# A fused attention and phase-mixer kernel: the first batch's exponentials transposed by TensorE instead of by DMA, and a new instruction order

## The chip, the cores and the metric

One core of a Trainium2 chip runs the whole program. The metric is the device time of one execution in microseconds (us). The engines are TensorE (PE in the rows, with its weight loads as PEld), VectorE (DVE), ScalarE (ACT), GpSimd (POOL) and SyncE (SP), whose queue here only issues DMAs.

## The reference

```python
# q, k, v: 8 batches x 8 heads x 576 x 64;  w_theta, w_ch: 512 x 512;  w_tok_r, w_tok_i: 576 x 576
scores = q @ k^T / sqrt(64)                      # row block i sees column blocks j <= i, blocks of 64
attn   = exp(scores - max) / (sum + 1e-9)
x      = attn @ v                                # per batch 576 x 512 after joining the heads
theta  = x @ w_theta
y      = w_tok_r @ (x * cos(theta)) + w_tok_i @ (x * sin(theta))
u      = x + y
out    = u + relu(u @ w_ch)
```

## The kernel before

The work is cut into some 3,400 parts: functions with the parts that they need, the PSUM banks that they take and the banks that they leave. `emit` calls them by a long list of numbers, `ORDER`; `BANKS` names a bank for each label that a part takes, and `PLACES` an engine (A, D or P for ACT, DVE, POOL) for each part that may run on several. Each engine works through its own instructions in this order, so a wait holds up all that stands behind it on that engine.

A batch has eight heads in four pairs; pair p holds heads 2p and 2p+1. A head's 576 query rows are five tiles: piece A is tiles 3, 2 and 4, piece B tiles 1 and 0, and for the first 16 heads the two pieces go separately, later as one. For the first three batches the scores are products of f32 operands (L589, `scores_wide` into two banks for each head, `scores_narrow` into one, and `scores_first`, L617, for tile 4), for the others three f16 products each.

A head then passes through: row maxima on DVE (L633); the bias `m` (L641, POOL or DVE); exponentials on ACT (L646) out of PSUM into an f32 tile `t` in SBUF, after which the score banks are free; `high`, a cast to f16 `p` (L431 on ACT, L433 on DVE or POOL); `low`, the rest t - p in f16 (L436, DVE or POOL); `turn`, a DMA transpose of both (L665, `pt<-p`, in SP's queue); the products with v (L680, PE); normalising on DVE (L692, L694, L698). `t` may be written again by the next pair when `low` has read it. DMAs (L686) join the halves of x; x is split (`xp`), transposed by DMA (L806) and multiplied with w_theta (L816, L819). The angles are reduced on ACT (L828) and DVE (L834, L440/L442), and one part, `sines`, turns a batch's angles into cosines and sines with six ACT instructions (L849, L851) between two ACT_TABLE_LOADs. Products with x (`z`, L860), their split into `zh` and `zl`, the token mix (L884), u (L893, L900), the channel mix (L907), relu (L913, L915), the sum (L923) and the store follow. All eight batches run interleaved: while one is mixed, the attention of the next is done.

The weights are loaded, scaled and split into high and low f16 parts during the first batch (lines L462 to L518). Loads of q, k and v (L772) stand in SP's queue among the transposes.

Of the kernel before, what the change touches and what calls it, by code (L numbers as in the profile page):

```python
# [12 lines left out]
F32 = mybir.dt.float32  # L13
# [20 lines left out]
HALVED = 8  # L34
WHOLE = 3

ORDER = [
# [191 lines left out]
    "DAAADAPPAPPPAPDPAPPDAPPPPPPDPPPPAPPPPPPDPPDDAPDADAPDDADDAAAADAAPPDAPPDDDDADPDAPDPADDDAPDPPDDPADPPDDDDAPDPPPPPDPP"  # L229
    "PADDADDPDPPDDADAAAA"  # L230
)

Part = namedtuple("Part", "f needs takes leaves on")


# [19 lines left out]
def attention_phase_mixer(  # L255
# [10 lines left out]
    nc = tc.nc  # L266
# [751 lines left out]
    def keys(name, n):  # L1018
        return [(name, n, x) for x in pieces(n)]
# [157 lines left out]
```

## Time and profile before

| | |
|---|---|
| time, median of 3 runs (lowest, highest) | 665.99 us (665.96, 668.66) |
| profiled execution: span | 668.2 us |
| busy PE | 615.9 us (92%) |
| busy DVE | 570.6 us (85%) |
| busy ACT | 508.4 us (76%) |
| busy POOL | 393.8 us (59%) |
| mean granted TensorE clock | 0.959 |

The page gives no separate own time for the profiled execution; its span of 668.2 us is 0.3% above the median of the runs, and only the run of 668.66 us could hold it. Sums below are made against the span. Busy shares are means over the whole execution; the stages, of which the first 124 us are very unlike the rest, are told apart in the rows below. In rows of a timeline the columns are start, duration, engine, line, operation, out<-in, shapes, count, and in brackets the idle time before it with what ended it.

### The profile page before, as it was taken

The page shows a single profiled execution, that of the slowest core. Times are in us where ns is not written, and L with a number is a line of the kernel's source. Part 1 is how long each engine was busy: PE and PEld are TensorE (multiplying, and loading weights), DVE is VectorE, ACT ScalarE, POOL GpSimd, SP SyncE. Part 2 cuts the span into 40 slices and gives each one's busy share as a digit, 9 for nine tenths or more (in the row PEclk, how much of TensorE's full clock was granted, in tenths as well). Part 3 has the DMA queues.
Part 4 walks back from the last instruction along what each step waited for, and adds up shares of the span by engine and source line. Part 5 has one row for each costly group of instructions (what it writes and reads, how often), then busy time and mean ns, then how long its engine had stood idle before and what let it go on. Part 6 is the DMA issues. An engine that isn't in the chain of part 4 may idle for free. (4 is left out here: it accounts for less than half of the span.)

```text
span 668.2 us, 18051 instructions
## 1 busy us (share of the span) xinstructions
PE 615.9 (92%) x7372; PEld 459.6 (69%) x7374; DVE 570.6 (85%) x1136; ACT 508.4 (76%) x776; POOL 393.8 (59%) x411
## 2 busy tenths in 40 slices
PE   5477796999999999999999998999999998999997
PEld 3155554876788578776778766875786586857775
DVE  4987897998998998989989889999998998846474
ACT  5997878776997998978998899889997986325111
POOL 4355564876575446564675748664777476673340
PEclk9578896999999999999999999999999998999999
DMA  8999999998989596989869897889797655840002
GB/s 347 381 235 231 207 165 196 248 197 147 233 197 214 126 242 122 194 170 183 220 169 169 164 222 164 192 169 202 186 207 156 120 89 117 172 82 1 19 36 88
DMA packets 268514, 116.57 MB, mean 174 GB/s; under 512 B 256016, under 2 KB 256016, under 8 KB 268432
## 3 DMA queue, kind: packets, MB, share of 16 engines
q1 hardware_dynamic: 268432, 115.43, 78.5%
q8 instruction: 57, 0.93, 0.6%
q14 instruction: 25, 0.20, 0.1%
HBM read 42.01 MB, written 9.44 MB: 77 GB/s over the span
## 5 line engine op out<-in xcount | busy, mean ns | idle before, releaser
L884 PEld LDWEIGHTS <-zh 128*128 128x128 f16 x1152 | 112.7, 98 | 30.4 <-issue 1.6
L884 PE MATMUL g<-wT_h,zh 128*128 128x288 f16 x405 | 115.9, 286 | 0.3 <-DVE xT L923 0.3
L884 PE MATMUL g<-wT_l,zh 128*128 128x288 f16 x405 | 115.8, 286 | 0.0
L884 PE MATMUL g<-wT_h,zl 128*128 128x288 f16 x405 | 115.8, 286 | 0.0
L680 PE MATMUL g<-v,pt 128*128 128x65 f16 x2880 | 104.8, 197 | 10.5 <-DVE xn L698 4.4
L680 PEld LDWEIGHTS <-pt 128*128 128x128 f16 x2880 | 101.0, 100 | 17.7 <-issue 9.6
L633 DVE TENSOR_REDUCE m<-s 128x1 f32<-128x576 f32 (+3 forms) x134 | 86.4, 668 | 12.0 <-PE s L596 11.8
L436 POOL TENSOR_TENSOR p<-t,p 128x512 f16<-128x512 f32 (+4 forms) x31 | 69.8, 2254 | 43.7 <-ACT p L431 26.5
L431 ACT CAST p<-t 128x1600 f16<-128x1600 f32 (+4 forms) x62 | 79.7, 1289 | 7.8 <-DMA pt<-p 6.8
L436 DVE TENSOR_TENSOR p<-t,p 128x1600 f16<-128x1600 f32 (+4 forms) x49 | 80.4, 1643 | 4.3 <-ACT p L431 3.8
L860 POOL TENSOR_TENSOR aa<-aa,xn 128x256 f32<-128x256 f32 (+1 forms) x63 | 51.5, 829 | 28.1 <-ACT aa L849 25.5
L816 PEld LDWEIGHTS <-xT 128*128 128x128 f16 x384 | 36.6, 98 | 43.8 <-DMA xT<-xp 2.4
L884 PEld LDWEIGHTS <-zl 128*128 128x128 f16 x576 | 56.4, 98 | 14.4 <-POOL m L641 0.4
L646 ACT ACTIVATE t<-s,m,size 128x576 f32<-128x576 f32 (+1 forms) x80 | 59.2, 777 | 8.1 <-POOL m L641 6.0
L907 PEld LDWEIGHTS <-wch_h 128*128 128x128 f16 x512 | 48.1, 98 | 14.7 <-issue 2.9
L633 DVE TENSOR_REDUCE m<-g 128x1 f32<-128x320 f32 (+2 forms) x154 | 53.5, 369 | 2.3 <-PE g L596 0.7
L646 ACT ACTIVATE t<-g,m,size 128x192 f32<-128x192 f32 (+2 forms) x100 | 49.2, 533 | 5.4 <-POOL m L641 3.5
L436 POOL TENSOR_TENSOR zl<-aa,zh 128x512 f16<-128x512 f32 (+1 forms) x38 | 44.7, 1181 | 12.9 <-PE g L617 6.9
L907 PE MATMUL g<-ul,wch_h 128*128 128x288 f16 x164 | 46.9, 286 | 2.8 <-DVE ul L900 2.8
L884 PE MATMUL s<-wT_l,zh 128*128 128x288 f16 x171 | 48.9, 286 | 0.0
L884 PE MATMUL s<-wT_h,zl 128*128 128x288 f16 x171 | 48.9, 286 | 0.0
L884 PE MATMUL s<-wT_h,zh 128*128 128x288 f16 x171 | 48.9, 286 | 0.0
(187 smaller groups left out, 1632.8 us busy)
## 6 DMA issues: line engine op xcount, KB each, us to landing
rv<-in_v SPq DMA_DIRECT2D x16, 768.0 KB, 5.3
rq<-in_q SPq DMA_DIRECT2D x16, 640.0 KB, 5.3
rk<-in_k SPq DMA_DIRECT2D x16, 576.0 KB, 5.5
out<-xT SPq DMA_DIRECT2D x32, 288.0 KB, 2.5
w_raw<-in_w_tok SPq DMA_DIRECT2D x5, 576.0 KB, 5.4
pt<-in_w_tok SPq DMA_DIRECT2D x4, 576.0 KB, 7.4
w_raw<-in_w_theta SPq DMA_DIRECT2D x4, 512.0 KB, 7.0
w_raw<-in_w_ch SPq DMA_DIRECT2D x4, 512.0 KB, 5.6
```

The lines of the kernel that those rows point to most:

```text
L431: nc.scalar.copy(out=out, in_=x)
L436: engine_of(on).tensor_tensor(out=out, in0=x, in1=y, op=ALU.subtract)
L633: nc.vector.tensor_reduce(out=self.m[:, i:i + 1], in_=self.scores_of(i), axis=AX.X, op=ALU.max)
L646: nc.scalar.activation(out=t_parts[self.hh][:, to:to + n], in_=self.scores_of(i), func=AF.Exp, scale=self.scales()[0], bias=self.m[:, NI + ...
L680: nc.tensor.matmul(o[:, i, :], lhsT=source[:, block, :], rhs=vv[:, slot, hh, :], start=first, stop=last)
L816: nc.tensor.matmul(g, lhsT=xT[:, xx + i, :], rhs=ww[:, dt, :], start=first, stop=last)
L860: engine_of(on).tensor_tensor(out=cd, in0=cd, in1=self.xns[dt][:, i0:i0 + ni, :], op=ALU.mult)
L884: nc.tensor.matmul(g, lhsT=zz[:, kk, cols], rhs=ww[:, kk, ts], start=(n == 0 and kk == k0 and nn == 0), stop=n == 4 and kk == k0 + ni - 1 ...
L907: nc.tensor.matmul(g[:, 0:HS], lhsT=ww[:, dt, e * P:(e + 1) * P], rhs=uu[:, dt, th * HS:(th + 1) * HS], start=dt == 0 and n == 0, stop=dt ...
```

## The change

For the eight heads of the first batch (`PE_TURNED = 8`) the casts, subtractions and DMA transposes of `high`, `low` and `turn` go (16, 16 and 16 of them). In their place stand `turn_up` (L670 after the change), which transposes the f32 exponentials in blocks of 128 x 128 on TensorE back into the head's own score banks, 8 blocks for piece A, 4 for B, and one more for tile 4 into a bank of its own (100 blocks in all); `turned_high` (20 casts from PSUM to the f16 `pt`, 19 on ACT, 1 on DVE) and `turned_low` (20 subtractions that read PSUM, all on DVE). The score banks of these heads are left by `turned_low`, not by the exponentials; `t` may be written again after the transposes. `sines` becomes six parts, and each part of `z` needs only the one or two whose result it reads. `ORDER`, `BANKS` and `PLACES` are new throughout.

```diff
+PE_TURNED = 8
...
 ORDER = [
-    8, 9, 158, 160, 335, 10, 11, 0, 1, 16, 17, 2, 56, 340, 364, 363, 372, 373, 374, 336, 339, 57, 40, 3, 350, 58,
...
-    t_parts = [const.tile([P, USED[hh]], F32, name=f"t{hh}") for hh in range(2)]
+    t_parts = [const.tile([P, NS[hh]], F32, name=f"t{hh}") for hh in range(2)]
+    nc.gpsimd.memset(t_parts[0][:, USED[0]:NS[0]], 0.0)
...
+        def turned_in(self, piece):
+            if piece == "4":
+                return bank_of["t4", self.n]
+            return self.pair.wide(self.hh) if piece == "A" else self.pair.narrow(self.hh)
+
+        def turn_up(self, piece):
+            x, to = t_parts[self.hh], self.turned_in(piece)
+            for j, c in enumerate({"A": range(CUT, CUT + 1024, P), "B": range(0, CUT, P), "4": [CUT + 1024]}[piece]):
+                nc.tensor.transpose(to[:, j * P:(j + 1) * P], x[:, c:c + P], ident)
...
+        def turned_high(self, piece, on):
+            x, hi, _ = self.turned_parts(piece)
+            copied(on, hi, x)
+
+        def turned_low(self, piece):
+            x, hi, lo = self.turned_parts(piece)
+            less("D", lo, x, hi)
...
-        def sines(self):
+        def sines(self, n):
...
-            for c, x, rows in ((a[:, 0:4, :], a[:, 0:4, :], slice(0, P)), (a[top, 4, left], a[top, 4, left], top),
+            if n in (0, 1):
+                steps = [(a[:, 2 * n:2 * n + 2, :], a[:, 2 * n:2 * n + 2, :], slice(0, P))]
...
-                    add(("e", n, i), step_of(h.exponentials, i), needs, leaves=leaves)
...
+                    add(("e", n, i), step_of(h.exponentials, i), needs, leaves=leaves if n >= PE_TURNED else ())
+                if n < PE_TURNED:
+                    for x in [piece] + ["4"] * (piece == "A" and hh == 0):
+                        done = [("e", n, i) for i in {"A": (3, 2), "B": (1, 0), "4": (4,)}[x]]
+                        add(("tp", n, x), step_of(h.turn_up, x), done, takes=[("t4", n)] if x == "4" else ())
+                        add(("th", n, x), step_of(h.turned_high, x), [("tp", n, x)] + w_free, on="AD")
+                        add(("tl", n, x), step_of(h.turned_low, x), [("th", n, x)],
+                            leaves={"A": [("s1", p, hh, k) for k in range(2)], "B": [("s2", p, hh)], "4": [("t4", n)]}[x])
...
-                    part("z", (hf, n, half), m.times_x, [("sines", b)], on="PD")
+                    part("z", (hf, n, half), m.times_x, [("sines", b, x) for x in ((0,), (3,), (1,), (4,), (2, 5))[n]], on="PD")
```

Before the first token mix, DVE's order also loses nine biases and eleven small operations on weights, sizes, v and x to other engines, and gains five products `z`.

On PE at the start of the program, between the first pair's scores and the second pair's, the order before goes from the first wide scores (in s0 and s1) through the mask straight to the second wide scores in the same banks:

```order
L596 MATMUL s0_109<-ones_119,mask_q_70 128x2x64
L596 MATMUL s1_110<-ones_119,mask_q_70 128x2x64
L589 MATMUL s0_109<-rk_154,rq_152 128x512
L589 MATMUL s1_110<-rk_154,rq_152 128x512
```

At the same place the order now has (t0 and t1 are the exponentials of the pair's two heads, g4 to g7 single banks):

```order
L595 MATMUL s1_111<-ones_120,mask_q_70 128x2x64
...
L670 MATMUL g4_112<-ident_r_79,t1_98 128x128 x4
L616 MATMUL g7_115<-rk_151,rq_153 128x64 x2
L670 MATMUL g6_114<-ident_r_79,t0_97 128x128 x4
...
L670 MATMUL s1_111<-ident_r_79,t1_98 128x128 x8
L670 MATMUL s0_110<-ident_r_79,t0_97 128x128 x8
L670 MATMUL g6_114<-ident_r_79,t0_97 128x128
L588 MATMUL s0_110<-rk_151,rq_153 128x512
L588 MATMUL s1_111<-rk_151,rq_153 128x512
```

The second pair's wide scores now stand behind 25 transposes and, through the banks, behind the casts and subtractions that read them.

In SP's queue, the program's first DMAs and the loads of q and k for the second half of the second batch stood so before (the numbers tell buffers apart; pt is what a DMA transpose of p writes):

```order
L462 DMA w_raw_128<-in_w_theta 128x1024
L772 DMA rq_152<-in_q 128x1280
L772 DMA rk_154<-in_k 128x1152
...
L806 DMA_TRANSPOSE xT_1124<-xp_1071 128x10x128
L665 DMA_TRANSPOSE pt10_105<-p1_100 128x16x128
L665 DMA_TRANSPOSE pt10_105<-p1_100 128x8x128
L772 DMA rq_1201<-in_q 128x1280
L772 DMA rk_1219<-in_k 128x1152
```

and stand so now, with nothing ahead of the first two and, between the start and the loads of rq_736 and rk_783, no transpose of any kind:

```order
L796 DMA rk_151<-in_k 128x1152
L796 DMA rq_153<-in_q 128x1280
L461 DMA w_raw_129<-in_w_theta 128x1024
...
L796 DMA rq_736<-in_q 128x1280
L710 DMA xn_709<-xn_709 64x64
L796 DMA rk_783<-in_k 128x1152
L710 DMA xn_709<-xn_709 64x64
L796 DMA rv_843<-in_v 128x1536
L830 DMA_TRANSPOSE xT_847<-xp_692 128x10x128
```

Both loads have moved from behind the transposes of the second batch's first pair to ahead of the first transpose of x.

On ACT the first batch's sines stood in one piece between two table loads:

```order
L849 ACT_TABLE_LOAD
L849 ACTIVATE aa<-aa,half_pi 128x2048
L849 ACTIVATE aa<-aa,half_pi 64x256 x2
L851 ACTIVATE rr<-rr 128x2048
L851 ACTIVATE aa<-rr 64x256 x2
L646 ACT_TABLE_LOAD
```

and now they stand between the same two loads in pieces, with two of the reductions (L439) among them:

```order
L881 ACT_TABLE_LOAD
L881 ACTIVATE rr<-rr 128x1024
L439 ACTIVATE aa<-rr 128x256
L439 ACTIVATE aa<-rr 128x512
L883 ACTIVATE aa<-aa,half_pi 128x1024
L881 ACTIVATE rr<-rr 128x1024
L883 ACTIVATE aa<-aa,half_pi 64x256 x2
L883 ACTIVATE aa<-aa,half_pi 128x1024
L881 ACTIVATE aa<-rr 64x256 x2
L645 ACT_TABLE_LOAD
```

A product `z` can follow each piece instead of the last one.

## Rows read from the trace of the kernel before

**Rows 1.** Stage, length, busy PE, PEld, DVE, ACT, POOL (instructions), clock, DMA share, GB/s.

```profile
0.00:40.00 40.00, 21.12 (x98) 13.09 (x101) 28.42 (x60) 29.95 (x52) 18.00 (x43) 0.75 0.95 338
40.00:80.00 40.00, 30.05 (x416) 23.22 (x413) 32.89 (x79) 32.82 (x58) 23.30 (x26) 0.83 1.18 235
80.00:124.00 44.00, 36.43 (x400) 25.02 (x401) 39.24 (x80) 34.75 (x56) 23.96 (x27) 0.81 0.90 190
124.00:300.00 176.00, 175.36 (x2218) 133.40 (x2217) 161.59 (x332) 148.75 (x225) 111.00 (x115) 1.00 0.91 187
300.00:420.00 120.00, 116.11 (x1538) 85.90 (x1537) 110.59 (x216) 107.78 (x160) 77.22 (x73) 1.00 0.83 185
420.00:560.00 140.00, 132.88 (x1725) 98.48 (x1724) 131.00 (x252) 119.92 (x176) 90.80 (x84) 0.99 0.78 157
```

**Rows 2.** PE's timeline up to the first token mix (L884).

```profile
7.61 0.87 PE L589 MATMUL g<-rk,rq 64*128 64x320 f32 x1 [7.61 <-DMA rk<-in_k]
...
23.76 4.11 PE L589 MATMUL s<-rk,rq 64*128 64x512 f32 x16 [7.17 <-ACT t L646]
...
106.59 4.11 PE L589 MATMUL s<-rk,rq 64*128 64x512 f32 x16 [3.43 <-DMA rk<-in_k]
...
118.89 2.17 PE L589 MATMUL s<-rk,rq 64*128 64x512 f32 x16
...
122.43 1.55 PE L680 MATMUL g<-v,pt 128*128 128x65 f16 x45
123.81 0.29 PE L884 MATMUL g<-wT_h,zh 128*128 128x288 f16 x1
```

**Rows 3.** SP's queue: starts, time taken to issue, and count.

```profile
0.74 0.40 SPq L462 DMA_DIRECT2D w_raw<-in_w_theta  x1
...
1.67 0.42 SPq L772 DMA_DIRECT2D rk<-in_k  x1
...
94.25 4.34 SPq L665 DMA_TRANSPOSE pt<-p  x2
99.28 0.42 SPq L772 DMA_DIRECT2D rk<-in_k  x1
```

**Rows 4.** Two other stretches, same columns as rows 1.

```profile
9.90:113.00 103.10, 74.50 (x757) 50.66 (x758) 88.30 (x192) 87.41 (x146) 55.11 (x57) 0.78 1.05 249
123.80:198.10 74.30, 73.88 (x909) 56.02 (x906) 68.80 (x142) 59.51 (x94) 52.25 (x54) 1.00 0.98 194
```

**Rows 5.** DVE's timeline, the last that the first token mix needs.

```profile
110.85 1.16 DVE L633 TENSOR_REDUCE m<-s 128x1 f32<-128x448 f32 x2 [3.57 <-PE s L596]
111.92 0.68 DVE L436 TENSOR_TENSOR p<-t,p 128x512 f16<-128x512 f32 x1
112.52 0.48 DVE L698 TENSOR_TENSOR xn<-g,r 128x320 f32<-128x320 f32 x1
```

**Rows 6.** Groups of DVE by shape, 0 to 124 us: busy time, mean ns.

```profile
L436 DVE TENSOR_TENSOR p<-t,p 128x1024 f16<-128x1024 f32 x4 | 5.0, 1249 | 0.1
L433 DVE CAST p<-t 128x1024 f16<-128x1024 f32 x2 | 1.4, 690 | 0.8 <-DMA pt<-p 0.8
L834 DVE SCALAR_TENSOR_TENSOR rr<-s,size,aa 128x512 f32<-128x512 f32 x1 | 0.7, 737 | 0.0
L641 DVE TENSOR_SCALAR m<-m 128x3 f32<-128x3 f32 x5 | 1.6, 326 | 0.1
L860 DVE TENSOR_TENSOR rr<-rr,xn 128x256 f32<-128x256 f32 x3 | 1.5, 505 | 0.0
```

**Rows 7.** ACT's timeline, first and last of the first batch's sines.

```profile
105.02 2.92 ACT L849 ACTIVATE aa<-aa,half_pi 128x2048 f32<-128x2048 f32 x3
...
109.89 0.85 ACT L851 ACTIVATE aa<-rr 64x256 f32<-64x256 f32 x2
```

**Rows 8.** PE's waits from 124 to 560 us: total, times, longest.

```profile
PE g L907 <- DVE ul L900: 2.8, 2, 2.6
PE s L907 <- ACT t L646: 2.5, 2, 1.9
```

More of the change, by code (lines that the diff above doesn't have):

```diff
@@ L34 @@
 HALVED = 8
+PE_TURNED = 8
 WHOLE = 3
 ORDER = [
[176 rows of a table removed]
[174 rows of a table added]
 ]
 BANKS = (
-    "4556164551001236001234501234601235601235401231001236501236401235401234601235601235601235601234501235401235401235"
-    "4012346012354012346012346012345012354012356012356012346012356012365012346012364012365012365246551650445606454041"
-    "6540151630666461566050425316646355451406665420444500465601466501605440544155446405425450164156455646416040451634"
-    "52245163452601620132435450513216524"
+    "6036634613301236460123451012346501235400123650123100123640123640123540123460123560123560123560123450123540123540"
+    "1235401234601235401234601234601234501235401235601235601234601235601236501234601236401236501236524650165044562445"
+    "1366654015041066656146605041531566625545056616403655450046560146652046315014405544561042543015410645564641503045"
+    "126452542562535304460316014405260435142"
@@ L220 @@
 )
 PLACES = (
-    "DAAPDAPAAADAAAAAAPDAPDAAPAAAAAPAAPAAPAAPAADAAPADAAAAPDPPPPDDDDAPPDAPPAPDDDDAPPDADPPPDAPPPPADADPAPPAPPPPAPADPPDDP"
-    "DDPPPDAPPAPPADPPDDPADPAPPADPAPADADPADDADPAPAPADDADPPAPPPDPPADPADAPADPADAADPADDAPAAPPADPAPAAADADPADPPADADPADAPADA"
-    "PPADAAADDDPAPAAADADDAPPPPPADDADAAPPAPDADAAPDPDPADAAPDADPPDAPAPADPADAAPDADPAPAAAPADPPDAAPPADPAPAAAPADPADAAAPADPDP"
-    "AAPPDDPAPAAPPAPPAPPPPPADDADPDAPADAPADDAAPPPDDDAPPPAPDPADPPAPPDAPPPAPDDAPPDAPPPPPPADPPDDPAADADAADADADAPPDAADADPPP"
-    "PDDPPPDPPPPAPPDAPDPADPPPPPPADPPADPPAPDADAPAPDAADAADDAAPAPAPDDDAAAAPDPPDPAPDDDPPDAPDPPDPPAPDPAPDPAPDDADPDPPPAPPDP"
@@ L227 @@
-    "PDAAADDDAAAPPPPPDDAAAADPDADPDAPPPPPDDPPPDPPPDAPPPAPDPAPPPAPDPPPPAPAPADADAAADDADAPAPAPPPDAAADDPAPPPPDPPAPPPAPPPAD"
-    "PPAPPDAPDPAPDDADPDPPPAPAPADADDDADADDAPADPPAPAADADPDPPPPPPPPPPDDADPPPDPPAPDDPDDDAPPDAPDPAPDAPPDDDADADAAAADPDAPAPA"
-    "DAAADAPPAPPPAPDPAPPDAPPPPPPDPPPPAPPPPPPDPPDDAPDADAPDDADDAAAADAAPPDAPPDDDDADPDAPDPADDDAPDPPDDPADPPDDDDAPDPPPPPDPP"
-    "PADDADDPDPPDDADAAAA"
+    "ADPPAPPAAPDPPDAPAAPAPDDPPAAPAPPAADAADAPPAAPAAPAAPAAAPADPAPAPAPPAAPAPADAAPAAPAPAPAPPAAPAPAPAADPDPAPPAPPADAPPPPPPP"
@@ new lines @@
+    "PDPAPPPADPADPADPAPAPAPDADPADDADAPADPADPPADPDPAPDDPADDPADPPDPAAPADPAPAAAPADPADAAADADPADPPAPADPADAAAPADPADAAAPDDPA"
+    "PAAADADPADPPAPADPADAPAPADPADAAAPADPPDAAPPADPADAPAPADPADAAAPADDAPAAAPADPPPAAPPDDPAPAAADADPADAAAPADPAPAAAPDPPADAAA"
+    "PPPPADPPAPADDAPPPPPAPADAAAAADDPDPPAPDDADDPADDPADDDAPDDAPDDADDDAPDPAPPDDAPAPPAADAAAAAAPAPPPDDDADADPPAPDDAPPDPPDPA"
+    "PDPPPDPADDDADPDPPDDADPPAPPADPPDDPAAAAADAAAPDPDPDDADADAPDAPPPAPPDAPDPAPPPAPPDAPPPADPDAPDPAPPDAPPAPAPPPDADAADDAAPP"
+    "APAPDDDDDADDPAPPPPPPPAPDPPPPDAPPPAPDDAPDPAPDPADPPADDPDAPAPDDAAAAADAAPADPDAPDDDAAPPPPDPPPPDAPDPPPPDADDPAPPPAPPPAP"
@@ L231 @@
+    "DPADPPAPDADPDAPADDDAAADAAPAPAPAPADDDDPPPDPPAPDDAPDPDPPDDDDPAPDPAPPDPDPPAPPPPDDADAPADAAADAADADAPAPAPDDDDADAPPPDDP"
+    "DPPDADPPADPDPPPPPPPDADPPPPPPPDDPADPDPAPAPPDAAAAAAADDPDADADDADDDDPDPDPAPDPAPDDPPPDAPDDAPDDADPPPPDDDDPPAPPADDDADAD"
+    "ADDADAA"
 )
@@ L661, in low, with turned_parts @@
             less(on, lo, x, hi)
+        def turned_in(self, piece):
[6 more added lines that the diff above has]
+                nc.tensor.transpose(to[:, j * P:(j + 1) * P], x[:, c:c + P], ident)
+        def turned_parts(self, piece):
+            n = {"A": 8, "B": 4, "4": 1}[piece]
+            _, _, to, room = extent(self.hh, "B" if piece == "B" else "A")
+            at_ = to // P + (8 if piece == "4" else 0)
+            x = self.turned_in(piece)[:, 0:n * P].rearrange("p (a c) -> p a c", c=P)
+            return (x,) + tuple(self.turned[:, at_ + y:at_ + y + n, :] for y in (0, room // P))
+        def turned_high(self, piece, on):
[4 more added lines that the diff above has]
+            less("D", lo, x, hi)
         def turn(self, piece):
@@ L846, in sines @@
             left, right = slice(0, HC), slice(HC, DM)
-            for c, x, rows in ((a[:, 0:4, :], a[:, 0:4, :], slice(0, P)), (a[top, 4, left], a[top, 4, left], top),
-                               (a[top, 4, right], a[low, 4, left], low)):
-                nc.scalar.activation(out=c, in_=x, func=AF.Sin, scale=-2.0 * math.pi, bias=half_pi[rows])
-            for s, x in ((r[:, 0:4, :], r[:, 0:4, :]), (a[low, 4, left], r[top, 4, left]), (a[low, 4, right], r[low, 4, left])):
-                nc.scalar.activation(out=s, in_=x, func=AF.Sin, scale=2.0 * math.pi)
+            if n in (0, 1):
+                steps = [(a[:, 2 * n:2 * n + 2, :], a[:, 2 * n:2 * n + 2, :], slice(0, P))]
+            elif n == 2:
+                steps = [(a[top, 4, left], a[top, 4, left], top), (a[top, 4, right], a[low, 4, left], low)]
+            elif n in (3, 4):
+                steps = [(r[:, 2 * n - 6:2 * n - 4, :], r[:, 2 * n - 6:2 * n - 4, :], None)]
+            else:
+                steps = [(a[low, 4, left], r[top, 4, left], None), (a[low, 4, right], r[low, 4, left], None)]
+            for to, x, rows in steps:
+                if rows is None:
+                    nc.scalar.activation(out=to, in_=x, func=AF.Sin, scale=2.0 * math.pi)
+                else:
+                    nc.scalar.activation(out=to, in_=x, func=AF.Sin, scale=-2.0 * math.pi, bias=half_pi[rows])
         Z_PIECES = [(0, 0, 2, 0), (1, 0, 2, 4), (0, 2, 2, 2), (1, 2, 2, 6), (0, 4, 1, 8)]
@@ L1049, in attention_phase_mixer, with gone, turned_of @@
             w_free, o_free = turn_of(f"pt{hh}", [x for m_ in (heads if hh == 0 else [n]) for x in keys("weighted", m_)], 2), turn_of("o", [("normalise", n, 2)])
+            def gone(n, piece, name):
+                if n < 0:
+                    return []
+                if n < PE_TURNED:
+                    return [("tp", n, x) for x in ("A", "B", "4") if ("tp", n, x) in parts and (piece in ("all", x) or (piece == "A" and x == "4"))] if name == "low" else []
+                return [(name, n, x) for x in pieces(n) if "all" in (x, piece) or x == piece]
+            def turned_of(n, piece):
+                if n < PE_TURNED:
+                    return [("tl", n, piece)] + [("tl", n, "4") for _ in range(piece == "A" and n % 2 == 0)]
+                return [("turn", n, piece)]
             for piece in pieces(n):
@@ L1053, in attention_phase_mixer @@
                 add(("mn", n, piece), step_of(h.bias, piece), known + [("m", n, i) for i in mine], on="DP")
-                same = [("low", n - 2, x) for x in (pieces(n - 2) if n > 1 else ()) if "all" in (x, piece) or x == piece]
+                same = gone(n - 2, piece, "low")
                 for i in mine:
@@ L1060, in attention_phase_mixer @@
                         needs = needs + ([("e", n, i + 1)] if i in (2, 0) else [])
-                    add(("e", n, i), step_of(h.exponentials, i), needs, leaves=leaves)
-                same = [("turn", n - 2, x) for x in (pieces(n - 2) if n > 1 else ()) if "all" in (x, piece) or x == piece]
-                add(("high", n, piece), step_of(h.high, piece), [("e", n, i) for i in mine] + same, on="ADP")
-                add(("low", n, piece), step_of(h.low, piece), [("high", n, piece)], on="PD" if piece == "B" else "DP")
-                add(("turn", n, piece), step_of(h.turn, piece), [("low", n, piece)] + w_free)
-                needs = [("turn", n, piece), ("v2", p)] + ([("turn", heads[0], piece)] if piece != "B" else []) + o_free
+                    add(("e", n, i), step_of(h.exponentials, i), needs, leaves=leaves if n >= PE_TURNED else ())
+                if n < PE_TURNED:
+                    for x in [piece] + ["4"] * (piece == "A" and hh == 0):
[4 more added lines that the diff above has]
+                            leaves={"A": [("s1", p, hh, k) for k in range(2)], "B": [("s2", p, hh)], "4": [("t4", n)]}[x])
+                else:
+                    same = gone(n - 2, piece, "turn")
+                    add(("high", n, piece), step_of(h.high, piece), [("e", n, i) for i in mine] + same, on="ADP")
+                    add(("low", n, piece), step_of(h.low, piece), [("high", n, piece)], on="PD" if piece == "B" else "DP")
+                    add(("turn", n, piece), step_of(h.turn, piece), [("low", n, piece)] + w_free)
+                needs = turned_of(n, piece) + [("v2", p)] + (turned_of(heads[0], piece) if piece != "B" else []) + o_free
                 add(("weighted", n, piece), step_of(h.weighted, piece), needs)
@@ L1089, in attention_phase_mixer @@
         a_free = turn_of("aa", [z for z in z_all if z[3] in (0, 2, 4)])
-        r_free = turn_of("rr", [z for z in z_all if z[3] in (1, 3)] + [("sines", b)])
+        r_free = turn_of("rr", [z for z in z_all if z[3] in (1, 3)] + [("sines", b, 5)])
         for i in range(NI):
@@ L1097, in attention_phase_mixer @@
             part("size", (i,), m.size, [("rest", b, i)], on="AD")
-        part("sines", (), m.sines, [("size", b, i) for i in range(NI)])
+        for n in range(6):
+            rows = [4] if n in (2, 5) else [2 * (n % 3), 2 * (n % 3) + 1]
+            part("sines", (n,), m.sines, [("size", b, i) for i in rows] + [("sines", b, 2) for _ in range(n == 5)])
         for hf in range(2):
```

349 rows, old and new, of the table ORDER are left out of this document.

## Prediction

> **What bounds the kernel now.** I read the busy table by stages first [rows 1], because the means of the whole execution hide two unlike parts. From 124 to 300 us PE is busy 175.36 of 176 us at a clock of 1.00: PE is the bound, and the other engines only have to keep up. From 300 to 420 it loses 3.9 us, from 420 to 560 7.1. In the first 124 us it is another kernel: PE is busy 21.12 + 30.05 + 36.43 = 87.6 us, so 36.4 us idle, and the granted clock is 0.75 to 0.83. There the reader should look at DVE: 28.42 + 32.89 + 39.24 = 100.6 of 124 us, and 39.24 of the last 44. ACT is near it (97.5). So the start is a chain through DVE and ACT, with the weights' preparation in between, and ends where the token mix begins, at 123.81 [rows 2]; after that PE has work without end.
>
> Second I read what PE waits for in the start [rows 2]: 7.61 us for the first load of k; 7.17 us before the second pair's scores, for the exponentials that have to leave its banks; 3.43 us at 103 us for a late load of k. That load was issued at 99.28, right behind two transposes that held SP's queue from 94.25 to 98.59 [rows 3]. DVE waits 3.57 us for the same scores [rows 5].
>
> Third I asked which DVE instruction the first mix needs last. By the order it is the normalising of head 10, at 112.52, done at 113.0 [rows 5]; behind it PE still has 10.8 us of its own queue (two pairs' scores, two heads' products) before the mix. Between DVE's first maximum at 9.90 and 113.0 it is busy 88.3 us and idle 14.8 [rows 4].
>
> **The change part by part.**
>
> *Loads.* The first k and q no longer stand behind a weight. k was issued at 1.67, the weight at 0.74 [rows 3]: q, now second, goes at about 1.2, 0.5 us earlier, and 512 KB less (128 x 1024 floats) are ahead of it, 1.5 us at the stage's 338 GB/s [rows 1]. Between 0.5 and 2.0 I take **-1.3 us**. The second batch's later q and k go ahead of the transposes, so DVE's 3.57 us wait should vanish: **-3.6** (nothing, if its scores are then late for another reason).
>
> *DVE's work.* Removed: 3 casts at 0.69 and 4 subtractions at 1.25 to 1.3, 7.2 us [rows 6]. Added: 8 subtractions of 1024 columns at 1.25, 8 of 512 that read PSUM at 0.74, 4 of 128 and a cast at some 0.35 each (an estimate below the 0.505 of 256 columns), together 17.7 [rows 6]. No row reads 1024 columns from PSUM in a subtraction; 2 x 0.74 is the upper bound, 1.8 us more in all. Net +10.5. Neighbouring instructions overlap: 111.92 + 0.68 is 112.60, the next starts at 112.52 [rows 5]; 0.07 on each of the 21 gives back 1.5. Nine biases less at about 0.25 (the row of three columns has 0.33) and eleven small operations less, five products of 0.505 more [rows 6], come to -2.2 - 3.2 + 2.5 (the eleven by the order and the means of their groups). Sum **+6.1 us** on DVE ahead of the first mix.
>
> *Where the chain now ends.* In the new order the last DVE instruction that the first mix needs stands directly ahead of it (a low part of z), where the old one had 10.8 us of PE work behind it. So I follow DVE: 113.0 - 1.3 - 3.6 + 6.1 = 114.2. The score banks of the first batch are now held through transposes, cast and subtraction. The next scores, and DVE's next maxima, queue behind these, where they waited for the exponentials only. One such cycle adds a 1024-column cast and subtraction, but DVE has weights to prepare meanwhile; I add one pair of subtractions, 1.25 + 0.74 = **+2.2** with a gap. In return `t` is free after the transposes and needs no longer wait for `low`, and the DMA transposes leave the path. First mix at **116.5** instead of 123.8: **-7.3 us**. Bounds: if DVE never waited, 113.0 - 14.8 - 1.3 + 6.1 = 103 (PE's queue does not allow it, see below); if each of the four pairs' cycles cost the whole cast, subtraction and transposes (some 4 us), 114.2 + 16 = 130.
>
> *PE's transposes.* 100 blocks of 128 x 128 in f32. No row shows one. Below: an f16 product takes 1.55/45 = 0.034 us [rows 2], 3 us in all. Above: f32 products of 1,024 columns take 2.17 us at 2.4 GHz and 4.11 at 1.2 [rows 2], with two products of half the rows side by side; a block of 128 columns is an eighth, 0.27 or 0.51, so 27 or 51 us. The operation passes data as the f32 product does, but there is one for each block: I take 0.2, **20 us**, hidden: PE has 87.6 + 20 = 107.6 us of work ahead of 116.5. The cover is gone above (116.5 - 87.6)/100 = 0.29 each; from there every 0.1 costs 10 us.
>
> The Trainium skill, "TensorE: Matmul & The Clock Gate", Part 4 (PE-mode transpose), gives about 390 ns for a bf16 block alone and about 275 ns inside a kernel, and says that full clock doesn't come from transposes. By 275 the sum is 27.5 us and changes nothing here; by 390 PE's work is 126.6 us, and the time some 10 us above my forecast. The granted clock of 0.75 to 0.83 in the start agrees that PE is not at full speed there; no row of before shows a transpose.
>
> *ACT.* 19 casts for 9 on nearly the same columns, in the place of casts on POOL and DVE, less weights: 87.6 to 89.7 us by the order and the rows' means, at 97.5 busy of 124 [rows 1] no new bound. *POOL* loses 15 of its subtractions: off the path. *SP* loses 16 transposes.
>
> *Sines.* The first batch's block runs from 105.02 to 110.7 [rows 7]. Products z could begin when the first cosines and sines are done, some 3 us earlier. Their engines are DVE, which is full, and POOL; I cost it at nothing. If DVE had room it would be -2.
>
> *Between first and second mix.* 123.8 to 198.1: PE 73.88 of 74.3, DVE 68.8 [rows 4]. By the order DVE gets another 5.8 us there: 74.6 of 74.3. At 93.6% DVE (420 to 560) PE lost 5.1%, at 92.2% (300 to 420) 3.2% [rows 1]. I take 3.4% of 74.3: **+2.5 us** back.
>
> *The rest.* Another 5.7 us of DVE (17.6 in the whole kernel) over 470 us, 44 us less on POOL. The named late waits, 2.8 us for a low part of u and 2.5 for exponentials behind a sine block [rows 8], will lie elsewhere; nothing, +-4.
>
> **Sum.** -7.3 + 2.5 = -4.8 us. The profiled span of 668.2 becomes 663.4; it lies 2.2 us above the median of the runs, so against 665.99 I forecast **661.2 us**.
>
> **Rivals.**
> 1. *Slower: DVE becomes the bound of the dense stretch.* From 124 to 560 us DVE is busy 403.2 of 436 (92.5%), and PE lost 11.7 there [rows 1]. With 11.5 more DVE is at 95.1%. If the loss of 420 to 560 (5.1%) holds over all of it, PE loses 22.2, 10.5 more; against a start only 4 better the time is 672. It decides once PE's idle time in this stretch passes 11.7 + 7.3 + 3.3 = 22. For it: the loss grows with DVE's share from stage to stage. Against: 124 to 300 had 91.8% and lost 0.6, so order matters more than share.
> 2. *Nothing measurable: the gain of the start is eaten* by the bank cycles (three more waits like the 7.17 us one) or by dear transposes. First mix at 120 to 124: 665 to 669, I say 667.
> 3. *A larger gain.* DVE's idle 14.8 us before 113 mostly goes, first mix near 111 (PE's 107.6 us of work is the floor), and the late waits stay as they are: 653.
>
> Chances: forecast 0.42 (its own range 657 to 665), rival 1 0.18, rival 2 0.20, rival 3 0.20. What a measurement can tell from no change is about 0.5%, 662.7 to 669.3. Faster: rival 3 and four fifths of the forecast, 0.53. Same: the rest of the forecast, most of rival 2 and some of rival 1, 0.27. Slower: the rest of rivals 1 and 2, 0.20. The range goes from rival 3 nearly to rival 1's price: **651 to 671**.
>
> **What would show it.** First scores at 6.3 us; no wait for k at 103; transposes at 0.2 us each with PE busy some 107 us before the first mix; that mix at 114 to 119; DVE over 85% busy up to it; the second batch's mix 75 to 78 us after the first; PE idle after it about as before. It is wrong if PE waits repeatedly for banks held by `turned_low`, if a transpose takes over 0.29 us, or if PE's gaps after 124 us sum to 20.

## The result and the profile after

The changed kernel takes **658.2 us** (median of 4 runs, 657.96 to 661.9); the kernel before, with the three runs of above and one more, 667.33 us (4 runs, 665.96 to 668.83). The medians lie 9.1 us apart; the ratio on record is 0.9887 with a 95% interval of 0.985 to 0.9924: 7.5 us faster (5 to 10). The forecast was 661.2 us.

The profiled span is 656.2 us, 12.0 below that of before. Not all of it is gain. The profiled run of after took 657.96 us, so a run's time is its span and 1.8 us; the profiled execution of before with its span of 668.2 us stood for a run of 670.0, not for the median.

Busy time by stages of the changed kernel, columns and stretches as in [rows 1]:

```profile
0.00:40.00 40.00, 25.09 (x195) 17.43 (x196) 30.96 (x66) 32.34 (x55) 15.05 (x48) 0.91 0.88 342
40.00:80.00 40.00, 37.52 (x512) 27.83 (x509) 39.67 (x94) 35.64 (x65) 22.29 (x32) 1.00 0.61 151
80.00:124.00 44.00, 38.30 (x453) 29.14 (x454) 41.24 (x96) 39.91 (x68) 24.42 (x26) 0.88 1.01 185
124.00:300.00 176.00, 175.57 (x2145) 127.25 (x2144) 162.59 (x318) 146.18 (x228) 93.93 (x98) 1.00 0.88 176
300.00:420.00 120.00, 117.13 (x1584) 89.10 (x1581) 113.62 (x225) 109.67 (x165) 73.65 (x77) 1.00 0.86 191
420.00:560.00 140.00, 135.69 (x1790) 100.06 (x1786) 129.97 (x255) 122.79 (x185) 88.32 (x78) 1.00 0.86 163
```

DVE, which was busy 32.89 of the 40 us from 40 to 80, is now busy 39.67 of them; DMA's share fell from 1.18 to 0.61. TensorE's timeline up to the first token mix (now L916), beside [rows 2]:

```profile
6.92 2.18 PE L588 MATMUL g<-rk,rq 64*128 64x320 f32 x12 [6.92 <-DMA rq<-in_q]
...
17.54 1.09 PE L670 MATMUL s<-ident_r,t 128*128 128x128 f32 x8 [0.52 <-ACT t L645]
...
24.00 4.11 PE L588 MATMUL s<-rk,rq 64*128 64x512 f32 x16 [1.87 <-DVE pt L435]
...
48.11 2.25 PE L670 MATMUL s<-ident_r,t 128*128 128x128 f32 x16 [0.20 <-ACT t L645]
...
98.93 2.64 PE L704 MATMUL g<-v,pt 128*128 128x65 f16 x45 [4.28 <-DVE xn L722]
...
110.62 0.30 PE L916 MATMUL g<-wT_h,zh 128*128 128x288 f16 x1
```

The first mix is at 110.62 us instead of 123.81, 13.2 us earlier. From there to the end it is 545.6 us against 544.4 (and 541.7 in a second execution of the kernel before, experiment 1): the rest of the kernel gives back 1 to 4 us, and the whole gain lies in the start. Where in the start, one row of each kernel tells: the stretch from 9.90 us, DVE's first maximum of before, to the first mix, first of before, then of after.

```profile
9.90:123.80 113.90, 85.12 (x897) 59.35 (x899) 98.62 (x214) 94.71 (x160) 62.12 (x67) 0.78 1.02 247
```

```profile
9.90:110.60 100.70, 84.54 (x1000) 61.21 (x996) 97.81 (x218) 93.49 (x164) 51.98 (x72) 0.92 0.81 220
```

The third busy time is DVE's. It does the same amount, 98.6 and 97.8 us. Its idle time went from 15.3 to 2.9 us, and that is 12.4 of the 13.2. TensorE, the first busy time, is as busy as before although the 100 transposes came on top; the granted clock rose from 0.78 to 0.92. The clock is a rival explanation, but it is not enough by itself: the second pair's wide scores take 4.11 us, at a granted clock of 0.50, in both kernels (at 23.76 and 24.00 us), and DVE waited 1.1 us for them before and 0.2 now. What the higher clock is worth alone no run shows. What DVE waited for then, and waits for now, in the same two stretches:

```profile
DVE m L633 <- PE s L596: 8.1, 6, 3.6
DVE p L436 <- ACT p L431: 2.8, 2, 1.9
```

```profile
DVE r L716 <- PE g L704: 1.4, 1, 1.4
DVE rr L858 <- ACT aa L852: 0.6, 2, 0.4
DVE m L632 <- PE s L595: 0.2, 1, 0.2
```

Of the six waits for scores, 8.1 us, one of 0.2 is left.

### The profile page after: what moved, and what is told of

It is laid out like the page before. It is cut to its first block, busy times and chain, and to the rows that moved or that the text cites. A ratio compares the mean times of both kernels' runs of the same rounds, so it can differ in the third digit from the quotient of the medians.

```text
span 656.2 us, 18226 instructions
## 1 busy us (share of the span) xinstructions
PE 620.3 (95%) x7474; PEld 459.1 (70%) x7474; DVE 578.4 (88%) x1153; ACT 511.3 (78%) x803; POOL 352.3 (54%) x392
## 5 line engine op out<-in xcount | busy, mean ns | idle before, releaser
L916 PEld LDWEIGHTS <-zh 128*128 128x128 f16 x1152 | 112.7, 98 | 31.5 <-issue 1.7
L916 PE MATMUL g<-wT_h,zh 128*128 128x288 f16 x396 | 113.4, 286 | 2.0 <-DVE xT L955 2.0
L916 PE MATMUL g<-wT_l,zh 128*128 128x288 f16 x396 | 113.2, 286 | 0.0
L916 PE MATMUL g<-wT_h,zl 128*128 128x288 f16 x396 | 113.2, 286 | 0.0
L704 PE MATMUL g<-v,pt 128*128 128x65 f16 x2880 | 100.9, 195 | 7.0 <-DVE xn L722 5.4
L704 PEld LDWEIGHTS <-pt 128*128 128x128 f16 x2880 | 97.4, 98 | 13.3 <-issue 4.5
L430 ACT CAST p<-t 128x1536 f16<-128x1536 f32 (+4 forms) x51 | 68.0, 1337 | 2.7 <-DMA pt<-p 2.0
L435 POOL TENSOR_TENSOR p<-t,p 128x1536 f16<-128x1536 f32 (+4 forms) x17 | 45.0, 2650 | 46.5 <-ACT p L430 32.0
L916 PEld LDWEIGHTS <-zl 128*128 128x128 f16 x576 | 56.4, 98 | 18.6 <-DVE zl L435 2.1
L632 DVE TENSOR_REDUCE m<-g 128x1 f32<-128x192 f32 (+2 forms) x156 | 54.1, 370 | 7.6 <-PE g L595 7.5
L645 ACT ACTIVATE t<-g,m,size 128x320 f32<-128x320 f32 (+2 forms) x100 | 49.4, 535 | 9.7 <-POOL m L640 9.1
L916 PE MATMUL s<-wT_h,zl 128*128 128x288 f16 x180 | 51.5, 286 | 1.8 <-DVE zl L435 1.8
L916 PE MATMUL s<-wT_h,zh 128*128 128x288 f16 x180 | 51.5, 286 | 0.0
L916 PE MATMUL s<-wT_l,zh 128*128 128x288 f16 x180 | 51.5, 286 | 0.0
L892 POOL TENSOR_TENSOR aa<-aa,xn 128x256 f32<-128x256 f32 (+1 forms) x58 | 43.6, 761 | 9.7 <-ACT aa L883 8.5
L939 PE MATMUL g<-uh,wch_h 128*128 128x288 f16 x160 | 45.8, 286 | 1.8 <-ACT t L645 1.2
```

The source lines that it names most:

```text
L430: nc.scalar.copy(out=out, in_=x)
L435: engine_of(on).tensor_tensor(out=out, in0=x, in1=y, op=ALU.subtract)
L632: nc.vector.tensor_reduce(out=self.m[:, i:i + 1], in_=self.scores_of(i), axis=AX.X, op=ALU.max)
L645: nc.scalar.activation(out=t_parts[self.hh][:, to:to + n], in_=self.scores_of(i), func=AF.Exp, scale=self.scales()[0], bias=self.m[:, NI + ...
L704: nc.tensor.matmul(o[:, i, :], lhsT=source[:, block, :], rhs=vv[:, slot, hh, :], start=first, stop=last)
L892: engine_of(on).tensor_tensor(out=cd, in0=cd, in1=self.xns[dt][:, i0:i0 + ni, :], op=ALU.mult)
```

## The experiments

Each kernel was run beside the kernel before on one chip; ratios are to that, so the change's own 0.9887 is the mark to compare with.

**1. The kernel before, once more.** No edit.

> The kernel before, unchanged, profiled once more. If the first profile (span 668.2 us) was typical, the span is again 667 to 669 us. If it was a late one, as the changed kernel's pair of 656.2 us span and about 658 us time hints, the span is near 664 us, and about 4 of the 12 us between the two profiles are no gain of the change.

Ratio 1.0015 (0.9994 to 1.0036), span 663.6 us: 4.6 below the first profile. First mix at 121.9 instead of 123.8; a further 2.5 us lie between 492 and 567. The ten runs here have spans of 663.6 to 668.3 us, of which the profiled one is the shortest. So the profile that the sum was made against was a late one, and this one is early; the span of a median run lies between them. The stretch from 9.90 us to the first mix in this execution, and DVE's waits for scores in it:

```profile
9.90:121.90 112.00, 81.02 (x897) 56.33 (x900) 100.20 (x214) 94.79 (x160) 62.93 (x67) 0.82 1.04 251
```

```profile
DVE m L633 <- PE s L596: 6.9, 5, 2.9
```

Against this execution the change makes the start 11.3 us shorter: 8.9 us of DVE's idle time (11.8 to 2.9) and 2.4 of its busy time. Behind the first mix it is 3.9 us longer. That DVE's idle time is most of the gain holds for both executions; how much of it, 12.4 or 8.9 us, does not.

**2. The loads alone, in the old order.** The order of SyncE's queue:

```diff
-L462 DMA w_raw<-in_w_theta 128x1024
-L772 DMA rq<-in_q 128x1280
 L772 DMA rk<-in_k 128x1152
+L772 DMA rq<-in_q 128x1280
+L462 DMA w_raw<-in_w_theta 128x1024
...
+L772 DMA rq<-in_q 128x1280
+L772 DMA rk<-in_k 128x1152
 L806 DMA_TRANSPOSE xT<-xp 128x10x128
```

> The kernel before with two pairs of loads moved in SyncE's queue: the first k and q ahead of the first weight, and the second batch's later q and k ahead of the first transpose of x; all else as it was. The prediction's two terms (1.3 and 3.6 us): 661 to 663 us, no wait for k near 103 us. The rival, that VectorE was late for other reasons: the wait moves to another cause and the time stays within 1.5 us of before.

Ratio 1.0033 (1.0011 to 1.0056): no gain, some 2 us slower. TensorE's waits up to its first mix at 124.1 us:

```profile
PE s L594 <- ACT t L651: 10.6, 2, 9.3
PE g L594 <- DMA rq<-in_q: 6.7, 1, 6.7
PE g L622 <- DVE xn L703: 5.3, 2, 4.2
```

The first load comes 0.9 us sooner and the late wait for k has gone. But the second pair's scores now wait 9.3 us for the exponentials where they waited 7.17, and at 113.8 us TensorE waits 4.2 for DVE. Both terms were real waits and neither was the one that ended last.

**3. The loads moved back, in the new order.** The reverse edit on the changed kernel.

> The changed kernel with its first q and k behind the first weight again, and the second batch's later q and k behind the transposes of that batch's first pair, as in the kernel before. The prediction's two terms (1.3 and 3.6 us), seen in the new order: 661 to 664 us, with a wait for k in the last 20 us before the first mix. Rival, as the move in the old order gave nothing: within 1.5 us of 658.

Ratio 1.0045 (1.0021 to 1.0068), 10 to 12 us slower than the changed kernel, more than either theory had; first mix at 122.4. The lines that make it, of TensorE, DVE's waits, and SyncE's queue:

```profile
95.01 0.66 PE L627 MATMUL g<-rk,rq 128*128 128x64 f32 x2 [9.57 <-DMA rk<-in_k]
```

```profile
DVE rr L869 <- ACT aa L863: 11.3, 4, 9.5
```

```profile
84.33 4.43 SPq L700 DMA_TRANSPOSE pt<-p  x1
88.81 0.57 SPq L807 DMA_DIRECT2D rq<-in_q  x1
89.44 0.89 SPq L807 DMA_DIRECT2D rk<-in_k  x2
```

k goes out at 89.4 us, behind a transpose; TensorE stands 9.57 us at a small score product, the theta products queue behind it, and with them ACT and DVE. So the same moves that were worth nothing in the old order are worth 10 to 12 us in the new one, which uses these scores earlier; the first load is 0.6 of it (TensorE's first wait is 7.5 us instead of 6.9).

**4. The sines alone, in the old order.** The six-part function, the parts issued one after the other where the one part was.

```diff
-        part("sines", (), m.sines, [("size", b, i) for i in range(NI)])
+        for n in range(6):
+            rows = [4] if n in (2, 5) else [2 * (n % 3), 2 * (n % 3) + 1]
+            part("sines", (n,), m.sines, [("size", b, i) for i in rows] + [("sines", b, 2) for _ in range(n == 5)])
```

> The kernel before with the sines in six parts, one behind the other at the old place; all else as before. The prediction's term of nothing: within 2 us of before. Rival, that the split itself shortens the start or the waits behind the sines in the later batches: 3 to 8 us less.

Ratio 0.9993 (0.9969 to 1.0016): nothing.

**5. The sines whole, in the new order.** All six instructions at the place of the last part, products z behind them.

```diff
         def sines(self, n):
+            if n != 5:
+                return
...
-                    part("z", (hf, n, half), m.times_x, [("sines", b, x) for x in ((0,), (3,), (1,), (4,), (2, 5))[n]], on="PD")
+                    part("z", (hf, n, half), m.times_x, [("sines", b, 5)], on="PD")
```

> The changed kernel with each batch's sines in one piece again, at the place of the last of the six parts, and the products z behind it; all else in the new order. The prediction's term of nothing for the split: within 2 us of 658. Rival, that the earlier products z are part of the shorter start (the first now starts 5 us ahead of the last sine): 661 to 664 us, first mix 3 to 6 us later.

Ratio 1.0411 (1.0362 to 1.0459), but not where either theory had it: the first mix stays at 110.9 us, and the later batches lose, 79.1, 73.9, 80.4 and 84.1 us from mix to mix against 75.1, 69.7, 77.4 and 74.3. DVE in the second batch:

```profile
168.87 0.43 DVE L896 TENSOR_TENSOR rr<-rr,xn 128x256 f32<-128x256 f32 x1 [2.37 <-ACT rr L887]
...
171.79 0.49 DVE L733 TENSOR_TENSOR xn<-g,r 128x320 f32<-128x320 f32 x1 [1.99 <-ACT t L656]
```

The new order puts z into DVE's queue where a part of the sines has just ended; with one block, DVE and all behind it wait for the block. Behind the first mix DVE waits 10.0 us for sines in four such places and 8.1 for exponentials behind them; how the rest of the loss divides is not shown. Part of it is my deferring of parts (170 places differ), so the size is an upper bound.

**6. The turning alone, in the old order.** Transposes at the old place of each cast, the subtraction from PSUM at that of the old one, parts put off where a bank is still held, sines whole.

```diff
+PE_TURNED = 8
...
         def sines(self, n):
+            if n != 0:
+                return
```

> The kernel before with the first batch turned by TensorE, in the order of before (each cast and subtraction at its old place, with the transposes ahead of the cast, tile 4 into whichever bank is free, parts put off only where a bank is still held), sines in one piece. Theory A, that the DMA transposes kept VectorE waiting in the start: at least half of the gain of the change, 658 to 662 us, VectorE's idle time before the first mix down from 14.8 to under 9 us. Theory B, that the gain is the new order's: within 2 us of before or slower, up to 672 us, since VectorE has 10 us more to do and the banks are held longer.

Ratio 1.088 (1.0846 to 1.0915), 59 us slower, far beyond theory B's 672 us, all of it in the start: first mix at 182.1 us. DVE waits there:

```profile
DVE pt L446 <- ACT pt L441: 24.0, 14, 4.6
DVE m L643 <- PE s L606: 19.6, 6, 4.3
```

This is rival 2's cycle, unhidden: scores wait for the subtraction, maxima for scores, the subtraction for the cast. The order here was not written for the turning, so the 59 us are the price in this order, not the least that an order of that kind could reach.

**7. The DMA transposes, in the new order.**

```diff
-PE_TURNED = 8
+PE_TURNED = 0
```

with `high`, `low` and `turn` at the places of `turned_high` and `turned_low`, on the engines of before.

> The changed kernel with the first batch turned by DMA as before (casts, subtractions and DMA transposes on the engines of before, at the places in the new order where cast and subtraction from PSUM stood; each DMA behind its subtraction), all else new. Theory A: most of the gain is gone, 664 us or more, with waits for DMA transposes in the first 110 us. Theory B: most of it stays, 658 to 661 us.

Ratio 1.0222 (1.0187 to 1.0257); first mix at 137.8. TensorE waits up to it:

```profile
PE g L626 <- DMA rq<-in_q: 11.2, 1, 11.2
PE g L714 <- DMA pt<-p: 10.1, 5, 2.9
PE g L714 <- DVE xn L732: 9.8, 3, 5.3
```

Transposes hold SyncE's queue again, and loads and products wait behind them. Theory A's figure and waits came here, and in experiment 6 theory B's direction. Read as one question, whether the gain is the turning's or the order's, neither answer holds: each alone, put into the other's order part by part, was slower than the kernel before, and only together did they gain. An order written for either alone was not tried.

**8. More work for DVE in the start, holding no bank.**

```diff
         def low_part(self):
             nc.vector.scalar_tensor_tensor(out=self.lo, in0=self.val, scalar=self.up, in1=self.hi, op0=ALU.mult, op1=ALU.subtract)
+            nc.vector.scalar_tensor_tensor(out=self.lo, in0=self.val, scalar=self.up, in1=self.hi, op0=ALU.mult, op1=ALU.subtract)
```

> The changed kernel with the 17 low parts of the weights computed twice on VectorE (same result; 13 of them, about 9.5 us, ahead of the first mix). It adds VectorE work that holds no bank. Theory A, VectorE bounds the start (idle only 3 of 101 us): 666 to 669 us, first mix near 120 us. Rival, the held banks or latencies bound it: at most 3 us more than 658.

**9. The subtractions twice.**

```diff
             less("D", lo, x, hi)
+            less("D", lo, x, hi)
```

> The changed kernel with the 20 subtractions out of PSUM made twice (same result; 15 to 16 us more on VectorE, and the score banks held so much longer). Theory A, VectorE's load: 14 to 17 us more, 672 to 675 us. Rival, the held banks: more than 18 us, since the four pairs' cycles lengthen while VectorE also works on.

**10. The transposes twice.**

```diff
                 nc.tensor.transpose(to[:, j * P:(j + 1) * P], x[:, c:c + P], ident)
+                nc.tensor.transpose(to[:, j * P:(j + 1) * P], x[:, c:c + P], ident)
```

> The changed kernel with all 100 transposes made twice (same result; 13.5 us more on TensorE at the measured 0.135 us each, and each bank filled later by 0.6 to 1.1 us). Theory A: hidden in TensorE's idle time, at most 3 us more, 658 to 661 us. Rival, the chain through the banks bounds the start: 8 to 14 us more.

The stretch from 9.90 us to the first mix in these three, in this order:

```profile
9.90:123.80 113.90, 86.53 (x996) 62.27 (x994) 111.87 (x224) 92.63 (x162) 55.57 (x71) 0.91 0.65 189
```

```profile
9.90:131.70 121.80, 89.10 (x996) 64.11 (x994) 115.17 (x237) 93.34 (x163) 52.93 (x72) 0.87 0.65 181
```

```profile
9.90:113.00 103.10, 89.81 (x1096) 69.69 (x1094) 97.63 (x217) 92.73 (x163) 52.29 (x72) 0.93 0.74 213
```

In 8 DVE is busy 14.1 us more (11.6 by the added instructions' own groups; the weights' other low parts also ran longer, 1.17 us a piece instead of 0.82) and the mix comes 13.2 us later, DVE idle 2.0: DVE's load bounds the start, nearly one for one. Ratio 1.0081 (1.0061 to 1.0102); at 673.2 us it is theory A's mechanism and beyond its range, as the added work was longer than reckoned. In 9 DVE is busy 17.4 us more and the mix 21.1 us later; the other 3.7 are idle time, in which waits for scores rose from 0.2 to 2.1, which is what the held banks show. Ratio 1.017 (1.0111 to 1.0229); past the rival's mark of 18 us, but most of it is DVE's work. In 10 the transposes take TensorE 24.7 us instead of 14.6, so 10.1 more and not the 13.5 that was expected, by these rows of the transposes alone, of the changed kernel and then of 10:

```profile
9.90:113.00 103.10, 14.61 (x100) 0.92 0.80 216
9.90:113.00 103.10, 24.74 (x200) 0.93 0.74 213
```

The mix is 2.4 us late, all of it DVE idle. Ratio 0.9901 (0.9873 to 0.9929): TensorE's transposes are hidden.

**11. More work for DVE after the second mix.**

```diff
-                nc.vector.tensor_tensor(out=m.xns[pair.pr][:, :, hh * D:(hh + 1) * D], in0=o[:, :, 0:D],
-                                        in1=self.r.unsqueeze(2).broadcast_to([P, NI, D]), op=ALU.mult)
+                for _ in range(2 if hh == 0 and self.n >= 16 else 1):
+                    nc.vector.tensor_tensor(out=m.xns[pair.pr][:, :, hh * D:(hh + 1) * D], in0=o[:, :, 0:D],
+                                            in1=self.r.unsqueeze(2).broadcast_to([P, NI, D]), op=ALU.mult)
```

> The changed kernel with the normalising of every second head from the third batch on made twice (same result; 24 x 0.49 us = 11.7 us more on VectorE, all behind the second mix). The prediction's rival 1, that VectorE is on the edge of bounding the dense stretch: 6 to 12 us more, with TensorE's idle time up by as much. The other reading, that VectorE there mostly waits for TensorE (18.2 us for the mix's banks alone): at most 3 us more, 658 to 661 us.

Ratio 0.9971 (0.995 to 0.9991): about 6 us slower than the changed kernel. From 124 us to the end, this kernel and then the changed one:

```profile
124.00:663.60 539.60, 522.71 (x6324) 385.57 (x6322) 480.02 (x925) 403.81 (x619) 287.19 (x288) 1.00 0.72 153
```

```profile
124.00:656.20 532.20, 519.38 (x6319) 384.68 (x6316) 466.48 (x899) 403.44 (x617) 290.50 (x287) 1.00 0.75 154
```

DVE does 13.5 us more and the stretch is 7.4 us longer; TensorE's idle time there rises by 4.1 us, from 12.8 to 16.9. Rival 1's mechanism is real: TensorE bounds this part, but DVE is so near that half of what is added there shows.

**12. Less for DVE in the start.** Nine parts to GpSimd, in the same order.

```diff
-    "ADPPAPPAAPDPPDAPAAPAPDDPPAAPAPPAADAADAPPAAPAAPAAPAAAPADPAPAPAPPAAPAPADAAPAAPAPAPAPPAAPAPAPAADPDPAPPAPPADAPPPPPPP"
+    "ADPPAPPAAPDPPDAPAAPAPPDPPAAPAPPAAPAAPAPPAAPAAPAAPAAAPADPAPAPAPPAAPAPAPAAPAAPAPAPAPPAAPAPAPAAPPDPAPPAPPAPAPPPPPPP"
```

(and two products z in a later line)

> The changed kernel with nine parts ahead of the first mix moved from VectorE to GpSimd, in the same order (three steps of the weights' split, two biases, a low part of x, one subtraction of 512 columns, two products z; about 4.4 us). Theory A, the start goes by VectorE's load, which a lone addition there showed at more than its own length: first mix 4 to 6 us earlier, 652 to 655 us. Rival, GpSimd is slower at each of them and the chain waits for it: 658 us or more.

Ratio 0.9905 (0.9872 to 0.9938): no better than the change. DVE has ten instructions fewer before the first mix at 111.6 us, but is as busy:

```profile
9.90:111.60 101.70, 83.44 (x999) 60.89 (x996) 97.43 (x208) 92.91 (x163) 60.13 (x81) 0.92 0.77 217
```

GpSimd's busy time rose by 8.2 us and DVE's mean instruction from 449 to 468 ns. The traces show where: the nine parts made 4.2 us on DVE, and three groups of instructions that stayed there, the same number in both kernels, ran some 3.2 us longer. Two of these groups up to the first mix, of the changed kernel and then of this one:

```profile
L572 DVE SCALAR_TENSOR_TENSOR v<-rv,size,v 128x768 f16<-128x768 f32 x7 | 7.4, 1053 | 0.0
L506 DVE SCALAR_TENSOR_TENSOR wT_l<-w_val,size_tok,wT_h 128x576 f16<-128x576 f32 x9 | 7.3, 819 | 0.0
```

```profile
L517 DVE SCALAR_TENSOR_TENSOR wT_l<-w_val,size_tok,wT_h 128x576 f16<-128x576 f32 x9 | 8.7, 978 | 1.0 <-ACT wT_h L433 1.0
L583 DVE SCALAR_TENSOR_TENSOR v<-rv,size,v 128x768 f16<-128x768 f32 x7 | 8.7, 1237 | 0.2 <-ACT v L433 0.2
```

The longest of them took 2.15 us and ran beside a low part of x (`xp`) that this experiment had moved to GpSimd; in the changed kernel the same instruction took 1.02:

```profile
80.36 1.02 DVE L572 SCALAR_TENSOR_TENSOR v<-rv,size,v 128x768 f16<-128x768 f32 x1
```

```profile
79.77 2.15 DVE L583 SCALAR_TENSOR_TENSOR v<-rv,size,v 128x768 f16<-128x768 f32 x1
79.07 2.03 POOL L446 TENSOR_TENSOR xp<-xn,xp 128x640 f16<-128x640 f32 x1
```

So what left DVE came back to it as longer instructions. In the four starts read for this (before, after, 8 and 12), every DVE instruction that ran over a fifth and 0.1 us longer than usual for its shape, 40 in all, ran beside a GpSimd instruction, though many others beside one ran at their usual length. No run isolates the cause. No version tried beats the changed kernel.

## Why the prediction was right, and where its steps failed

The direction and the place were right: the start is a chain through DVE, the dense stretch keeps its length, and the first mix moves. Step by step:

- **The base of the sum.** I took the profiled span to lie 2.2 us above the median. By after's pair of span and time it stood for 670.0 us, 4.0 above. Sums against one late execution carry its lateness; experiment 1's execution is as early as this one was late.
- **First load, -1.3:** -0.7. **Transposes, 20 us hidden:** 14.6 us for the 100, one starting 0.109 us after another within a row of them; hidden, as experiment 10 shows.
- **Late q and k, -3.6:** the size was wrong and so was the thought that it is a term by itself. Nothing in the old order, 10 to 12 us in the new (experiments 2 and 3).
- **DVE's work, +6.1:** from 88.3 to the 113.0 us mark of before [rows 4] to 97.8 now, +9.5. The eight wide subtractions cost 1.22 and the narrow ones 0.68 us, no more from PSUM than from SBUF.
- **DVE's idle time, the step that failed:** I kept 13.4 of the 14.8 us, taking off 3.6 for the late k and adding 2.2 for the held banks. Only 2.9 are left. About half of the 14.8 were waits for scores, of which I took off only the 3.6 us of the late load. This is what rival 3 described (first mix near 111); it had a chance of 0.20. The error in the start, 5.9 us, is this term (10.5) less the 3.4 us by which DVE's work was sized too small and the 1.3 us that moving the first load did not give at that mark.
- **Between first and second mix, +2.5:** 75.1 us against 74.3, +0.8. DVE is busy 69.6 there, where the order's count gave 74.6. Behind the first mix as a whole it is 1.2 us more than in the first execution of before and 3.9 more than in the second.
- **The sines, nothing:** right for the start and for the old order. That the new order leans on the parts in later batches (experiment 5) I had not seen.
- **The held banks:** rival 2's mechanism, in an order not written for it, costs some 58 us (experiment 6). The new order hides nearly all of it; in the profile after, DVE has something else ready for all but 2.9 of the 100.7 us.

In span the kernel came out 7.2 us below the forecast of 663.4, 5.9 in the start and 1.3 behind it; in time only 3.0 us below, because I went from span to time by taking 2.2 us off, where a run's time is its span and 1.8 us more. Two errors of opposite sign, of which the range of 651 to 671 held the sum: that the forecast lies so near is in part luck. The direction, the place and the bounding engine were not luck.

The Trainium skill, "TensorE: Matmul & The Clock Gate", Part 4, gives about 275 ns for a PE-mode transpose of a bf16 block in a kernel. The records here agree with that as the length of one (272 to 329 ns, f32), but within a row one starts 0.109 us after another, and the sum goes by this. So it reads in experiment 10:

```profile
48.34 0.27 PE L671 MATMUL s<-ident_r,t 128*128 128x128 f32 x1
48.45 0.27 PE L670 MATMUL s<-ident_r,t 128*128 128x128 f32 x1
48.56 0.27 PE L671 MATMUL s<-ident_r,t 128*128 128x128 f32 x1
```

The page also says that full clock does not come from transposes. Here the granted clock is 1.00, the 2.4 GHz level, from 40 to 80 us, where 50 of the 100 stand among score and weighted products, against 0.83 before. In experiment 10, 40 transposes stand in a row from 48.18 to 52.49 us, and the granted clock, at 1.00 ahead of them, stays there; no run shows it rise on transposes alone.

## What to carry to other kernels

Look for the engine that paces a start-up chain and split its time into work and waiting; if an order or a queue can be changed, price the waiting as something that may vanish as a whole, and the work as the floor. A new mechanism and the order written for it have one price together: either one alone, carried over part by part, was 15 to 59 us slower than the kernel before here. Before a sum is made against a profile, check what run it stands for: two executions of one kernel lay 4.6 us apart. Moving work to an idle engine is not free of the busy one: in experiment 12 the work that left VectorE came back as longer instructions beside GpSimd's.

## What was not expected of the hardware

Transposes of 128 x 128 f32 blocks through TensorE start every 0.109 us within a row, less than half of what the f32 product rows of before suggested as the upper bound at full clock (0.27). A subtraction of 1024 columns that reads PSUM took DVE 1.22 us, as one from SBUF did (1.25).
